# Eight output stores of the last batch on two queues instead of one

## The chip, the cores and the metric

The kernel runs on one core of a Trainium2 chip. The metric is the device time of one execution in microseconds (us), smaller being better. A core has TensorE (matrix products, "PE" in the profile, with its weight loads as "PEld"), VectorE (DVE), ScalarE (ACT), GpSimd (POOL) and SyncE (SP), each with its own instruction queue, and 16 DMA engines that carry out the transfers which these queues issue. A "q" behind an engine's name in the profile (SPq, ACTq) marks an instruction that its queue handles itself, such as the issue of a transfer.

## The reference

The inputs are q, k and v with the shape (8 batches, 8 heads, 576 positions, 64). A linear attention with an exponential feature map comes first, then a Fourier mixing over positions and channels, a normalisation and a two-layer network with a residual:

```python
q_p, k_p = (phi(q), phi(k))            # exp(proj - max|proj|), exp(-proj - max|proj|)
kv = np.einsum('bhsf,bhsd->bhfd', k_p, v)
z = np.sum(k_p, axis=2)
num = np.einsum('bhsf,bhfd->bhsd', q_p, kv)
den = np.einsum('bhsf,bhf->bhs', q_p, z)[..., None] + 1e-06
attn = num / den                       # then heads joined: x of (8, 576, 512)
mixed = np.real(fft(fft(x, axis=1), axis=2))
u = x + mixed
un = (u - mean(u)) / np.sqrt(var(u) + 1e-06)
out = u + np.maximum(un @ w_ch1, 0.0) @ w_ch2
```

The output is (8, 576, 512) in float32. Only its last line and its way to memory matter for the change.

## The kernel before, in words

The kernel goes through the eight batches as a software pipeline. Each kind of work is a generator ("stream"), and the string PLAN, one letter for a step, says in which order the steps are written into the program; each engine runs its own instructions in that order. The letter F is `forward`, the two-layer network, and PLAN ends in a run of F alone: the network of the last batch has nothing left to be mixed with.

The 576 rows of a batch are held as five chunks, `c` = 0 to 4: four of 128 rows, and chunk 4 of 64. They are not in the order of the output: because the mixing pairs row n with row 576 - n, some chunks hold rows in pairs and blocks in reverse. The tile `U` (named `X` in the profile, since it is the same tile) has the shape [128, 5, 513] and holds u; the result is added into it in place.

`forward(b)` runs in this order:

- `hidden(0, 256)`: the first layer for the positions of chunks 0 and 2; its matmuls are line 1222, and ScalarE applies the rectifier to `HT` (lines 1227 and 1229).
- `output(0)` and `output(2)`: the second layer, 16 accumulating matmuls a chunk at line 1239, then one VectorE instruction at line 1245, which scales the sum and adds it to `U`, then `store`.
- `hidden(256, S)` for the other positions, then `output(1)` and `output(3)`.
- Chunk 4. In the last batch (`b == B - 1`) its 512 columns are done as two halves of 256 (lines 1262 to 1281), each with two VectorE additions at line 1273 and two stores: 63 rows at line 1279, from ScalarE's queue for the first half and from SyncE's for the second, and one row at line 1280 from ScalarE's queue.

`store(b, U, c)` (lines 1197 to 1209) does nothing for chunk 0. For chunk 1 it stores chunks 0 and 1 together, since their rows alternate in the output: eight transfers at line 1200, one for each block of 16 partitions, each with 32 output rows of 2048 bytes (64 KB). Chunks 2 and 3 are one transfer of 256 KB each at line 1206. All of these are issued from `nc.sync`, SyncE's queue. A queue starts its instructions strictly in order: one that waits for its data, or is being issued, holds up everything behind it. Each store also has a counter that it raises when it lands; there are eight of these for the queues of SyncE and ScalarE, they are used in turn, and a store that takes one again waits until the earlier transfer with it has landed. The program ends when SyncE has seen all stores land (line 1403 in the profile) and the engines have met at a barrier.

Of the kernel before, what the change touches and what calls it, by code (L numbers as in the profile page):

```python
# [40 lines left out]
def kernel(  # L41
# [10 lines left out]
    nc = tc.nc  # L52
    B, H, S, D = q.shape
# [1143 lines left out]
    def store(b, U, c):  # L1197
        if c == 1:
            for a in range(8):
                nc.sync.dma_start(  # L1200
                    out=out[b, 225 - 32 * a:257 - 32 * a, :].rearrange("(r j) n -> r j n", j=2),
                    in_=U[16 * a:16 * a + 16, 0:2, 0:C],
                )
        elif c in (2, 3):
            rows_ = out[b, 320:576, :].rearrange("(a r j) n -> a r j n", r=16, j=2)
            nc.sync.dma_start(out=rows_[:, ::-1, 3 - c, :], in_=U[:, c, 0:C])
        elif c == 4:
            nc.sync.dma_start(out=out[b, 257:320, :], in_=U[1:64, 4, 0:C])
            nc.sync.dma_start(out=out[b, 0:1, :], in_=U[0:1, 4, 0:C])

    def forward(b):
# [23 lines left out]
        def output(c):  # L1235
            at = PLACE[c]
            po = pb.tile([128, C], F32, tag="pb", name="pso")
            for hh in range(NHH):
                nc.tensor.matmul(  # L1239
                    po[:], lhsT=HT[:, hh, at:at + 128], rhs=W2b[:, hh, :],  # L1240
                    start=(hh == 0), stop=(hh == NHH - 1),
                )
                if hh % 2 and hh < NHH - 1:
                    yield
            nc.vector.scalar_tensor_tensor(  # L1245
                out=U[:, c, 0:C], in0=po[:], scalar=scale_of[b, c], in1=U[:, c, 0:C],
                op0=ALU.mult, op1=ALU.add,
            )
            store(b, U, c)
            yield  # L1250
# [41 lines left out]
        for g in (0, 64):  # L1292
            nc.vector.scalar_tensor_tensor(
                out=U[0:64, 4, 0:C], in0=po[g:g + 64, :], scalar=scale_of[b, 4][0:64],
                in1=U[0:64, 4, 0:C], op0=ALU.mult, op1=ALU.add,
            )
        store(b, U, 4)
        yield

# [108 lines left out]
```

## Time and profile before

| what | value |
|---|---|
| time, median of 3 runs | 426.88 us (426.83 to 427.21) |
| profiled execution, its span | 426.9 us |
| TensorE matmul, busy | 400.0 us (94%) |
| TensorE weight load, busy | 255.6 us (60%) |
| VectorE, busy | 331.5 us (78%) |
| ScalarE, busy | 306.2 us (72%) |
| GpSimd, busy | 207.5 us (49%) |
| granted TensorE clock, mean | 0.993 |
| stores at line 1200 | 64, on SyncE's queue, 64 KB, 0.58 / 0.59 / 1.76 us (shortest, median, longest) |
| stores at line 1206 | 16, on SyncE's queue, 256 KB, 0.65 / 0.67 / 0.70 us |

The span reaches from the first to the last instruction of the program. Busy shares are averages over the whole span; what happens at the end of the program has to be read from the end. The time of a store here is that of its issue by the queue, not of its transfer.

### The profile page before, as it was taken

The numbers are of one execution on the slowest core, as the hardware profiler recorded it, in microseconds if no ns is written. First come the engines' busy times: TensorE is split into PE (matmuls) and PEld (weight loads), VectorE is DVE, ScalarE is ACT, GpSimd is POOL, SyncE is SP. The second block draws the span as 40 slices with busy tenths as digits, with TensorE's granted clock in tenths as the row PEclk, the third lists the DMA queues.
The fourth block names the chain that finished last, engine by engine and source line by source line (L and its number), as shares of the span: only waits on it lengthen the run. The fifth ranks groups of instructions, "written<-read, shape, count | busy, mean of one in ns | idle before, by whom it ended". The sixth has DMA issues, their size and how long they took to land.

```text
span 426.9 us, 10423 instructions
## 1 busy us (share of the span) xinstructions
PE 400.0 (94%) x4122; PEld 255.6 (60%) x4122; DVE 331.5 (78%) x682; ACT 306.2 (72%) x626; POOL 207.5 (49%) x271
## 2 busy tenths in 40 slices
PE   7787788999899999999899999999999999999993
PEld 3464466744676558555675558565766577657562
DVE  5989689698979986998779885898989786967102
ACT  7877699757984899499847888588868886353450
POOL 7983578635646077706673283734755332401000
PEclk9999899999999999999999999999999999999998
DMA  8999949993569458862899059754894151104204
GB/s 224 197 165 180 138 75 154 146 99 71 85 103 171 80 101 106 120 88 48 112 154 134 4 100 136 118 69 74 114 130 76 22 104 21 27 0 79 67 23 86
DMA packets 108699, 42.70 MB, mean 100 GB/s; under 512 B 82859, under 2 KB 103595, under 8 KB 108651
## 3 DMA queue, kind: packets, MB, share of 16 engines
q0 software_dynamic: 45936, 16.60, 36.2%
q1 hardware_dynamic: 62479, 25.31, 33.8%
q8 instruction: 32, 0.52, 0.5%
q10 hardware_dynamic: 236, 0.13, 0.1%
q14 instruction: 16, 0.13, 0.1%
HBM read 36.77 MB, written 9.44 MB: 108 GB/s over the span
## 4 chain that ended last, share of the span: by engine, by line
PE 57%; DVE 25%; ACT 8%; POOL 5%; issue 2%; DMA 2%; DVEq 0%; ACTq 0%; POOLq 0%
PE psf L1222 19%; PE pso L1239 19%; DVE R L903 4%; DVE cb L999 3%; PE kv L887 3%; DVE tg L994 3%; DVE MK L511 2%; PE pso L1286 2%; PE psD L1045 2%; PE pu L1104 2%; DMA UT<-UN 2%; DVE CEO L1034 1%; DVE MQ L555 1%; PE psq L547 1%; PE idle L1339 1%
## 5 line engine op out<-in xcount | busy, mean ns | idle before, releaser
L1222 PE MATMUL psf<-UT,W1b 128*128 128x320 bf16 (+1 forms) x1024 | 142.5, 286 | 3.2 <-DMA UT<-UN 1.5
L1239 PE MATMUL pso<-W2b,HT 128*128 128x512 bf16 x512 | 124.7, 379 | 0.0
L1222 PEld LDWEIGHTS <-W1b 128*128 128x128 bf16 x1024 | 94.0, 98 | 30.4 <-issue 4.7
L1239 PEld LDWEIGHTS <-HT 128*128 128x128 bf16 x512 | 46.4, 98 | 46.4 <-issue 2.6
L1227 ACT ACTIVATE HT<-psf 128x320 bf16<-128x320 f32 x128 | 53.5, 443 | 27.0 <-PE psf L1222 21.6
L1002 POOL TENSOR_TENSOR X<-cb,rd 128x320 f32<-128x320 f32 x56 | 41.4, 743 | 41.1 <-DVE rd L1001 39.4
L466 POOL TENSOR_TENSOR VCn<-VS,VCn 128x512 bf16<-128x512 bf16 x28 | 29.7, 1060 | 38.2 <-ACT VCn L461 35.4
L1229 ACT ACTIVATE HT<-psf 128x512 bf16<-128x512 f32 x64 | 38.0, 604 | 13.2 <-PE psf L1222 12.6
L555 DVE TENSOR_REDUCE MQ<-psq 128x8 f32<-128x1024 f32 (+1 forms) x32 | 34.3, 1085 | 14.1 <-PE psq L547 13.8
L1245 DVE SCALAR_TENSOR_TENSOR X<-pso,rs,X 128x512 f32<-128x512 f32 x32 | 23.6, 736 | 24.3 <-PE pso L1239 24.3
L497 ACT ACTIVATE KPn<-psk 128x1024 bf16<-128x1024 f32 x28 | 28.6, 1020 | 14.1 <-DVE MK L511 14.0
L497 ACT ACTIVATE KPp<-psk 128x1024 bf16<-128x1024 f32 x28 | 28.7, 1025 | 11.2 <-PE psk L491 11.1
L451 POOL TENSOR_TENSOR V4N<-VS,V4N 64x256 bf16<-64x256 bf16 x14 | 8.7, 622 | 56.1 <-ACT V4N L447 55.6
L511 DVE TENSOR_REDUCE MK<-psk 128x8 f32<-128x1024 f32 x28 | 33.9, 1213 | 1.0 <-ACT KPp L497 0.7
L1094 DVE TENSOR_TENSOR X<-pu,X 128x512 f32<-128x512 f32 (+3 forms) x49 | 23.3, 526 | 11.2 <-PE pu L1104 8.9
L466 POOL TENSOR_TENSOR VCp<-VS,VCp 128x512 bf16<-128x512 bf16 x28 | 29.6, 1058 | 0.0
L606 ACT ACTIVATE QPHP<-psh 128x1024 bf16<-128x1024 f32 x28 | 28.9, 1031 | 0.8 <-PE psh L597 0.6
L606 ACT ACTIVATE QPHN<-psh 128x1024 bf16<-128x1024 f32 x28 | 29.0, 1036 | 0.0
L1150 ACT ACTIVATE UN<-X,MV 128x512 bf16<-128x512 f32 (+1 forms) x35 | 24.5, 723 | 5.4 <-DVE MV L1175 3.1
L1174 DVE BATCH_NORM_STATS2 st<-X 128x6 f32<-128x512 f32 (+1 forms) x40 | 27.1, 677 | 0.3
L1190 POOL TENSOR_TENSOR rs<-VE,mhalf 128x5 f32<-128x5 f32 (+1 forms) x9 | 10.3, 1141 | 29.1 <-DVE VE L1189 29.1
L987 PEld LDWEIGHTS <-QPHP 128*128 128x128 bf16 x280 | 21.2, 99 | 4.6 <-DVE cb L999 1.0
(465 smaller groups left out, 819.5 us busy)
## 6 DMA issues: line engine op xcount, KB each, us to landing
out_dram<-X SPq DMA_DIRECT2D x16, 256.0 KB
out_dram<-X SPq DMA_DIRECT2D x64, 64.0 KB
QS<-in_q_dram POOLq DMA_DIRECT2D x14, 256.0 KB, 6.3
KS<-in_k_dram POOLq DMA_DIRECT2D x7, 512.0 KB, 7.5
VS<-in_v_dram POOLq DMA_DIRECT2D x14, 256.0 KB, 5.2
W1b<-in_moe_w_ch_dram POOLq DMA_DIRECT2D x1, 2048.0 KB, 13.1
W2b<-in_moe_w_ch_dram POOLq DMA_DIRECT2D x1, 2048.0 KB, 16.1
W2b<-in_k_dram SPq DMA_DIRECT2D x2, 512.0 KB
```

Of the source, the lines that this page charges most:

```text
L466: nc.gpsimd.tensor_tensor(out=VC[:, hs, :, 0:D], in0=values[b][0][:, hs, :].rearrange("p h (j d) -> p h j d", d=D), in1=VC[:, hs, :, D:D + ...
L497: nc.scalar.activation(out=KP[:, hs, :, :].rearrange("p e (jp jj) f -> p jj (e jp) f", jj=2), in_=psk[:], func=AT.Exp, scale=sgn,)
L511: nc.vector.tensor_reduce(out=MK[:, 2 * pr:2 * pr + 2, :].rearrange("p e (jp jj) -> p jj (e jp)", jj=2), in_=tiles[pr][:], axis=AX.X, op=A ...
L555: nc.vector.tensor_reduce(out=o, in_=i[:], axis=AX.X, op=ALU.max, apply_absolute_value=True)
L606: nc.scalar.activation(out=o, in_=psh[:], func=AT.Exp, scale=sgn)
L1002: nc.gpsimd.tensor_tensor(out=X[:, :, D * h:D * h + D], in0=cb[:, :, 0:D], in1=rd[:].to_broadcast([128, 5, D]), op=ALU.mult,)
L1150: nc.scalar.activation(out=UN[0:M, c, :], in_=X[0:M, c, 0:C], func=AT.Identity, scale=-1.0, bias=mv[0:M, c, 0:1],)
L1174: nc.vector.bn_stats(out=st[0:M, :], in_=X[0:M, c, 0:C])
L1222: nc.tensor.matmul(ps, lhsT=W1b[:, cc, 128 * hh:128 * hh + 128], rhs=UT[:, cc, lo:hi], start=(cc == 0), stop=(cc == NCC - 1),)
L1227: nc.scalar.activation(out=HT[:, hh, lo:hi], in_=ps, func=AT.Relu, scale=-1.0)
L1229: nc.scalar.activation(out=HT[:, hh - 1:hh + 1, lo:hi], in_=psw[:].rearrange("p (a n) -> p a n", a=2), func=AT.Relu, scale=-1.0,)
L1239: nc.tensor.matmul(po[:], lhsT=HT[:, hh, at:at + 128], rhs=W2b[:, hh, :], start=(hh == 0), stop=(hh == NHH - 1),)
```

## The change

In the last batch, the eight stores of chunk 1 are issued in turn by SyncE's queue (a = 0, 2, 4, 6) and ScalarE's queue (a = 1, 3, 5, 7). Sources, destinations and sizes are as before, and so are the stores of the seven other batches.

```diff
     def store(b, U, c):
         if c == 1:
             for a in range(8):
-                nc.sync.dma_start(
+                queue = nc.scalar if b == B - 1 and a % 2 else nc.sync
+                queue.dma_start(
                     out=out[b, 225 - 32 * a:257 - 32 * a, :].rearrange("(r j) n -> r j n", j=2),
                     in_=U[16 * a:16 * a + 16, 0:2, 0:C],
                 )
```

## The prediction, made before the changed kernel was run

> **What bounds the kernel now.** I read the chain of waits first. It runs on TensorE almost to the end, and the last compute is four short VectorE additions.
>
> ```profile
> 411.66 6.91 PE pso L1239 x32
> 418.57 1.01 PE pso L1266 x16
> ...
> 421.21 0.49 DVE X L1273
> ```
>
> The chain ends at 421.70 us, but the span is 426.9 us. The last 5.2 us hold no compute, only stores, so the timeline of that stretch comes next (columns: start, duration, engine, line, operation, count).
>
> ```profile
> 411.70 0.44 ACT L1227 ACTIVATE HT<-psf 128x320 bf16<-128x320 f32 x1
> ...
> 415.22 0.75 DVE L1245 SCALAR_TENSOR_TENSOR X<-pso,rs,X 128x512 f32<-128x512 f32 x1 [11.39 <-PE pso L1239]
> 416.00 5.11 SPq L1200 DMA_DIRECT2D out_dram<-X  x8
> ...
> 418.67 0.75 DVE L1245 SCALAR_TENSOR_TENSOR X<-pso,rs,X 128x512 f32<-128x512 f32 x1 [2.70 <-PE pso L1239]
> 419.67 2.03 DVE L1273 SCALAR_TENSOR_TENSOR X<-pso,rs,X 64x256 f32<-64x256 f32 x4 [0.25 <-PE pso L1266]
> 420.70 0.56 ACTq L1279 DMA_DIRECT2D out_dram<-X  x1
> 421.21 0.65 SPq L1206 DMA_DIRECT2D out_dram<-X  x1
> 421.30 0.67 ACTq L1280 DMA_DIRECT2D out_dram<-X  x2
> 422.63 0.31 SPq L1279 DMA_DIRECT2D out_dram<-X  x1
> ```
>
> SP issues the eight chunk 1 stores without a break from 416.00 to 421.11. Chunk 3 (the second L1245 row) is ready at 418.67 + 0.75 = 419.42, but its store sits behind them and starts at 421.21: **1.79 us lost in SP's queue**. The queue's own waits name one more thing:
>
> ```profile
> SPq L1403 <- DMA out_dram<-X: 2.5, 2, 2.2
> SPq L1279 <- DMA out_dram<-X: 0.7, 1, 0.7
> ```
>
> L1403 is the end of the program: SP stands there 2.2 us for a store to land, so transfers set the end. The second row says that SP's last store (chunk 4, second half) also waited 0.7 us for another output store. Last, the stretches of the tail (the last two numbers are the busy share of the 16 DMA engines and GB/s):
>
> ```profile
> 405.10:406.50 1.40, 1.40 (x13) 1.01 (x11) 0.00 (x0) 1.11 (x3) 0.00 (x0) 1.00 0.43 54
> 406.50:407.75 1.25, 1.25 (x11) 0.91 (x10) 0.00 (x0) 1.04 (x3) 0.00 (x0) 1.00 0.40 149
> ...
> 417.00:422.00 5.00, 3.43 (x40) 2.15 (x37) 2.68 (x5) 0.00 (x0) 0.00 (x0) 1.00 0.60 105
> 422.00:422.60 0.60, 0.00 (x0) 0.00 (x0) 0.00 (x0) 0.00 (x0) 0.00 (x0) 1.00 0.58 144
> 422.60:423.40 0.80, 0.00 (x0) 0.00 (x0) 0.00 (x0) 0.00 (x0) 0.00 (x0) 1.00 0.49 44
> 423.40:424.40 1.00, 0.00 (x0) 0.00 (x0) 0.00 (x0) 0.00 (x0) 0.00 (x0) 0.94 0.47 144
> 424.40:425.40 1.00, 0.00 (x0) 0.00 (x0) 0.00 (x0) 0.00 (x0) 0.00 (x0) 0.50 0.36 130
> 425.40:426.90 1.50, 0.00 (x0) 0.00 (x0) 0.00 (x0) 0.00 (x0) 0.00 (x0) 0.50 0.00 0
> ```
>
> The first two rows are chunk 2's store alone, issued at 403.89 with its last packet before 407.75. In the packet records that is 3.84 us from issue to the last 2048-byte packet. Chunk 3's store, of the same shape, takes 421.21 to 425.04, or 3.83 us: although chunk 1's packets run until 422.8, they cost it nothing. SP's last store is drained behind it, 0.30 us later (425.34). After that come 1.5 us without a packet (write receipts and the closing barrier), which I hold fixed. So the end today is chunk 3's issue + 3.83 + 0.30 + 1.5.
>
> **The change, step by step.** In the last batch four of the eight chunk 1 stores (a = 1, 3, 5, 7) move from SP to ACT. Batches 0 to 6 keep their order. The same 512 KB goes to the same places.
>
> 1. SP's queue. Eight issues at a pitch of (5.11 - 0.60) / 7 = 0.64 us become four: 416.00 + 3 x 0.64 + 0.59 = 418.5. SP is then free before chunk 3 is ready. Its store issues at 419.42 + 0.04 (the gap seen between 415.97 and 416.00, rounded up) = 419.46, **1.75 us earlier**. What is late next is the chunk 3 addition itself, 0.9 us after SP is free.
>
> 2. ACT's queue. ACT's last ACTIVATE ends at 412.14, and its next work is L1279 at 420.70, held by VectorE. Four stores go into this gap. No row shows this store on ACT. Nearest is ACT's w_phi load at L339, 64 rows, 0.56 and 0.61 us, and the same store on SP, 0.58 to 0.65. From below it is 0.23 (ACT's one-row store, L1280); from above 1.76, the longest of SP's 64 stores at L1200. I take 0.61 + 0.05: done at 418.6, with 2.1 us to spare before L1279. If that cover were gone (over 1.17 us a store), L1279 and both L1280 would slip by the excess. At 1.76 the four end at 423.2 and L1279 starts 2.5 us late; its last packet, 1.5 us after issue today (420.70 to 422.21), comes at 424.7, and the gain shrinks to 0.6.
>
> 3. SP's last store (L1279, second half) is held today until 422.63 by another output store, although its data is ready at 419.67 + 2.03 = 421.70. The order in which stores share completion counters shifts, so this wait may go (issue 421.73) or stay (422.63). I take that it goes; if it stays, the first packet comes 0.8 us later, as L1279's on ACT did, still no later than chunk 3's last packet plus 0.3. Worth 0.0 to 0.2.
>
> 4. Do the eight stores themselves finish in time? Here a rule speaks against the change. **The row:** from 417 to 422 the engines are busy 0.60 and move 105 GB/s, and SP offers 64 KB per 0.64 us, 102 GB/s. The engines follow the issue rate and are 40% idle. Mean packet time is 2048 B x 0.60 x 16 / 105 GB/s = 187 ns, so 256 packets need 256 x 0.187 / 16 = 3.0 us of all engines: from the first packet at 417.3 they could end at 420.3. **The rule:** the Trainium skill, "DMA: Bandwidth & Descriptors", section "Rules for kernel authors", says that spreading DMAs over SP, ACT and GpSimd gives no bandwidth, because all run on the same 16 engines, and saves only issue time, which it calls usually small beside the transfer. If 105 GB/s were all there is, the eight would still run to 422.3, chunk 3 would queue behind them, and the end would be 426.5 to 426.9. The row gives 425.4. I go by the row: issue is 5.11 us here, not small, and with ACT's L1279 beside SP's stores (422.00 to 422.60) the rate was 144 GB/s. A single store reads 16 partitions, and 64 KB in 0.6 us could also be a limit of their SBUF ports; the skill's "SBUF — State Buffer", section "Door 1", gives neighbouring blocks of 16 partitions different ports, so a pair, one per queue, would not share them. No run here shows that.
>
> 5. Chunk 3 then sends its first packets near 420.7, after or just at the end of the eight, and its last at 419.46 + 3.83 = 423.29. New beside it: ACT's first L1279, whose packets (421.5 to 422.2) today lie beside chunk 1's. It puts 7 packets of 46 ns on each of the engines that chunk 3 uses: +0.32. Then SP's last store, +0.30 as today: 423.91. TensorE and VectorE are untouched.
>
> Sum: 425.34 becomes 423.91, so 426.9 - 1.43 = 425.47; a part of step 5's 0.32 may fall into idle engine time, so I say **425.4**. The span equals the median of the runs shown (426.88), so nothing is added.
>
> **The rivals.**
>
> - *A: the engines are the bound, not the queue.* The eight stores drain at 105 GB/s whatever issues them, chunk 3's packets wait behind them until 422.3, and the time is 426.5 to 426.9. For it: the rule above, and SP's pitch and the moved bytes fit too well to tell apart. Against: 0.60 busy, 144 GB/s with two queues.
>
> - *B (slower): two queues at once slow each other's packets.* Chunk 3's first packets took 2048 x 0.49 x 16 / 44 = 365 ns (422.60 to 423.40), twice chunk 1's mean[...]. If all 256 packets of chunk 1 took X, they would end at 417.3 + 16X; at 0.33 us that is today's 422.6, and slower by 0.85 us begins at 0.38. At 0.40 chunk 3 queues 1.1 us longer: 428.0. Against: today's two-queue stretch got faster.
>
> - *C: larger gain.* If chunk 3 and the small stores interleave without cost, only SP's last store sets the end: issue 421.73 + 1.5 us to its last packet (as L1279 on ACT) = 423.2, so 426.9 - 2.1 = 424.8. This is the floor, set by VectorE.
>
> - *D: nothing moves, because another instruction holds ACT's queue.* The timeline shows none between 412.14 and 420.70; the time would be 426.9. I count it with A.
>
> **How the numbers follow.** Forecast 0.70 (425.0 to 425.9: step 5's addition at zero and ACT's stores at about 1.5 us), C 0.06, A and D 0.18, B 0.06. About 0.85 us (0.2%) is what a measurement of this kernel can tell from no change. The forecast and C are faster (0.76), A and D are the same (0.18), B is slower (0.06). The range reaches from C's floor, 424.8, into A to 426.7.
>
> **What would show it.** Right: four L1200 issues on SP and four on ACT ending near 418.6; L1206 at 419.46; DMA share in 417.3 to 420.5 above 0.8 at some 170 GB/s; the last packet near 423.9. Wrong: L1206 starting later than 420, ACT stores over 1.2 us each, or 417 to 422 still at 105 GB/s (A), or packet means over 330 ns there (B).

## The result and the profile after

| | before | after |
|---|---|---|
| time, median | 427.50 us (426.32 to 428.85, 22 runs) | 426.24 us (424.91 to 427.29, 22 runs) |
| profiled execution, span | 426.9 us | 424.3 us |
| start of the chunk 1 addition | 415.22 us | 414.05 us |
| from there to the end of the span ("the tail") | 11.65 us | 10.23 us |

The ratio of the times is 0.9965, with a 95% interval from 0.9955 to 0.9976: the change wins 1.0 to 1.9 us, 1.5 in the middle (the two medians differ by 1.26). The forecast was 425.4 within 424.8 to 426.7, and faster by 1.5.

Two things must be kept apart in this table. First, a time is not a span: the profiled execution after took 426.19 us for its span of 424.3, and in the 22 runs after 1.9 to 2.0 us lie outside the span. For the kernel before it is 1.8 us (its second profile: 427.25 for 425.5), so a tenth of the gain in the span is lost outside it, which these profiles don't explain. Second, the two profiles differ by 2.6 us, but 1.17 of that arises before the chunk 1 addition, where both programs are the same. Over the fourteen profiles of this study that addition starts anywhere from 412.66 to 415.22 us. So the tail is the measure from here on: it starts at the last event that the change can't touch. A second profile of the kernel before gave 11.54, one of the changed kernel 10.23 again, so it repeats to about 0.1 us.

The chain of waits after still ends in VectorE's short additions, at 420.52 us, with 3.8 us of stores behind them (5.2 before):

```profile
417.39 1.01 PE pso L1267 x16
...
420.04 0.48 DVE X L1274
```

The timeline of the tail after (line numbers are one higher from the changed line on; columns are start, duration, engine, line, operation, count):

```profile
414.05 0.75 DVE L1246 SCALAR_TENSOR_TENSOR X<-pso,rs,X 128x512 f32<-128x512 f32 x1 [11.39 <-PE pso L1240]
414.82 2.56 SPq L1201 DMA_DIRECT2D out_dram<-X  x4
414.83 2.86 ACTq L1201 DMA_DIRECT2D out_dram<-X  x4
...
417.50 0.75 DVE L1246 SCALAR_TENSOR_TENSOR X<-pso,rs,X 128x512 f32<-128x512 f32 x1 [2.70 <-PE pso L1240]
418.28 0.65 SPq L1207 DMA_DIRECT2D out_dram<-X  x1
418.50 2.03 DVE L1274 SCALAR_TENSOR_TENSOR X<-pso,rs,X 64x256 f32<-64x256 f32 x4 [0.25 <-PE pso L1267]
419.53 0.57 ACTq L1280 DMA_DIRECT2D out_dram<-X  x1
420.14 0.65 ACTq L1281 DMA_DIRECT2D out_dram<-X  x2
420.55 0.31 SPq L1280 DMA_DIRECT2D out_dram<-X  x1
```

SP and ACT issue four stores each, side by side. SP is idle from 417.38, and chunk 3's store starts 0.03 us after its addition ends. Measured from the start of the chunk 1 addition, it started at 5.99 us before and starts at 4.23 now: 1.76 us earlier. SP's last store has moved from 7.41 to 6.50. What it waits for has changed too, as the waits of SP's queue after say:

```profile
SPq L1404 <- DMA out_dram<-X: 1.9, 2, 1.5
SPq L1280 <- DVE X L1274: 1.5, 1, 1.5
```

It no longer waits for another store but for its data. The stretches of the tail after (the last two columns are the share of the DMA engines and GB/s):

```profile
416.10:419.10 3.00, 3.00 (x38) 2.06 (x36) 1.32 (x3) 0.00 (x0) 0.00 (x0) 1.00 0.79 175
419.10:419.50 0.40, 0.16 (x4) 0.00 (x0) 0.40 (x1) 0.00 (x0) 0.00 (x0) 1.00 0.00 0
419.50:420.50 1.00, 0.00 (x0) 0.00 (x0) 0.94 (x2) 0.00 (x0) 0.00 (x0) 1.00 0.46 53
420.50:421.50 1.00, 0.00 (x0) 0.00 (x0) 0.02 (x1) 0.00 (x0) 0.00 (x0) 1.00 0.50 147
421.50:422.10 0.60, 0.00 (x0) 0.00 (x0) 0.00 (x0) 0.00 (x0) 0.00 (x0) 1.00 0.56 205
422.10:422.80 0.70, 0.00 (x0) 0.00 (x0) 0.00 (x0) 0.00 (x0) 0.00 (x0) 1.00 0.29 100
422.80:424.30 1.50, 0.00 (x0) 0.00 (x0) 0.00 (x0) 0.00 (x0) 0.00 (x0) 0.78 0.00 0
```

The first row holds all eight chunk 1 stores: 175 GB/s in place of 105, so they are through in 3.0 us. The second row is a gap without a packet. The next three are chunk 3's store, slow at first and then fast as before (no run here shows why its first packets are slow), with the small stores of chunk 4 setting in from 7.12 us after the start of the chunk 1 addition; then come the rest of the small stores and the same 1.5 us to the end.

### The profile page after: what moved, and what is told of

Its sections match the earlier page's. It is cut to its first block, busy times and chain, and to the rows that moved or that the text cites. A ratio compares the mean times of both kernels' runs of the same rounds, so it can differ in the third digit from the quotient of the medians.

```text
span 424.3 us, 10395 instructions
## 1 busy us (share of the span) xinstructions
PE 399.3 (94%) x4093; PEld 255.9 (60%) x4122; DVE 330.8 (78%) x682; ACT 306.0 (72%) x626; POOL 207.8 (49%) x271
## 4 chain that ended last, share of the span: by engine, by line
PE 63%; DVE 22%; ACT 9%; DMA 2%; issue 2%; POOL 0%; DVEq 0%; ACTq 0%
PE psf L1223 21%; PE pso L1240 19%; DVE R L903 3%; DVE cb L999 3%; PE kv L887 3%; PE idle L1340 3%; DVE tg L994 3%; PE psD L1045 2%; DMA UT<-UN 2%; PE pso L1287 2%; PE pu L1104 2%; PE psq L547 1%; DVE MK L511 1%; PE psk L491 1%; PE psh L597 1%
## 5 line engine op out<-in xcount | busy, mean ns | idle before, releaser
L1240 PE MATMUL pso<-W2b,HT 128*128 128x512 bf16 x483 | 120.6, 379 | 1.7 <-issue 0.5
```

Of the source, the lines that this page charges most:

```text
L1240: nc.tensor.matmul(po[:], lhsT=HT[:, hh, at:at + 128], rhs=W2b[:, hh, :], start=(hh == 0), stop=(hh == NHH - 1),)
```

## The experiments

Twelve more runs were made, one profile each; with the two profiles above that makes fourteen, of eleven kernels. The main theory (Q in the expectations) says that the gain is chunk 3's store leaving SP's queue earlier. All times in this table count from the start of the chunk 1 addition. The third column is from the start of chunk 3's store to the end of its last 2048-byte packet; columns three and four come from the trace's packet records, which name the queue of a packet but not its store; packets are given to stores in the order of their queue.

| kernel | chunk 3's store starts | its transfer | last packet of all | tail |
|---|---|---|---|---|
| before, two profiles | 5.99, 5.99 | 3.83, 3.74 | 10.12, 10.03 | 11.65, 11.54 |
| one store on ACT | 5.43 | 3.69 | 9.42 | 10.96 |
| two on ACT, two profiles | 4.81, 4.83 | 4.39, 4.41 | 9.80, 9.85 | 11.31, 11.36 |
| three on ACT | 5.05 | 4.54 | 10.07 | 11.57 |
| after (four on ACT), two profiles | 4.23, 4.23 | 3.85, 3.85 | 8.68, 8.68 | 10.23, 10.23 |
| four on ACT, pairs 32 partitions apart | 4.23 | 3.81 | 8.65 | 10.20 |
| four on ACT, pairs 64 partitions apart | 4.23 | 3.85 | 8.69 | 10.25 |
| after, without chunk 4's first store | 4.23 | 3.80 | 8.40 | 9.96 |
| chunk 3 on ACT, all eight on SP | 4.24 | 4.45 | 11.43 | 12.92 |
| chunk 3 on POOL, all eight on SP | 4.82 | 4.83 (4096-byte) | 10.38 | 11.95 |
| after, and chunk 3 on POOL | 4.82 | 4.12 (4096-byte) | 9.50 | 11.19 |

**The two kernels again.**

> The changed kernel a second time, for a second profile. Tail means the time from the start of VectorE's chunk 1 addition to the end of the span: 11.7 us before (426.9 - 415.22), 10.2 us after (424.3 - 414.05). Theory Q (the gain is chunk 3's store leaving SP's queue earlier): the tail is 10.2 again within 0.1, and the start of the chunk 1 addition, which comes ahead of everything that was changed, may lie anywhere from 413 to 417. Rival N (the gain in the profile is mostly variation between executions): the tail moves as much as the start does.

> The kernel before a second time. Theory Q: tail 11.7 within 0.1, chunk 3's store again about 6.0 us after the start of the chunk 1 addition. Rival N: the tail varies by over 0.5 us.

Rival N falls: the tails repeat (10.23; 11.54 against 11.65), while the chunk 1 addition started at 413.26 and 413.94 us. Q holds for the changed kernel and for the start of chunk 3's store (5.99 again); the 11.54 lies 0.06 outside its 11.7 within 0.1.

**One, two and three stores on ACT.**

```diff
-                queue = nc.scalar if b == B - 1 and a % 2 else nc.sync
+                queue = nc.scalar if b == B - 1 and a in (7,) else nc.sync      # one
+                queue = nc.scalar if b == B - 1 and a in (5, 7) else nc.sync    # two
+                queue = nc.scalar if b == B - 1 and a in (3, 5, 7) else nc.sync # three
```

> One of the eight stores (a = 7) on ACT, seven on SP. Theory Q: SP is free 0.64 us earlier than before, so chunk 3's store starts 5.3 us after the start of the chunk 1 addition instead of 6.0, and the tail follows: 11.0 to 11.3. Rival L (what was won is the wait of SP's last store for an earlier store's counter): the tail falls to 10.8 (11.7 less that store's 0.9 us delay) if that wait is gone here, wherever chunk 3's store starts, and stays at 11.7 if it is not. Rival D (the data, not the queue): 11.7.

> Two of the eight stores (a = 5 and 7) on ACT, six on SP. Theory Q: chunk 3's store starts 4.7 us after the start of the chunk 1 addition, 1.3 us earlier than before, and the tail is 10.4 to 10.7. Rival L: 10.8 or 11.7, the same as with one store moved. Rival D: about 11.3, half of the way from before to after in steps of the stores moved (11.7 less 2/4 of 1.45 is 11.0 at the least).

> The kernel with two stores (a = 5 and 7) on ACT once more. Its first run started chunk 3's store at 4.8 us and yet had a tail of 11.3 us, because that store took 4.4 us to its last packet and not 3.8. Theory Q with a chance delay: this time 3.8 us and tail 10.7 to 10.8. Theory M (meeting: chunk 3's first, slow packets start while SP's last chunk 1 packets and ACT's small store are arriving, and this costs half a microsecond each time): 4.4 us and tail 11.3 again.

> Three of the eight (a = 3, 5, 7) on ACT, five on SP. SP is free at about 4.0 us after the start of the chunk 1 addition, before chunk 3 is ready. Theory Q: chunk 3's store starts at 4.2 us, as with four moved, and the tail is 10.2 to 10.3: the fourth store moved is worth nothing. Theory M: chunk 1's last packets on SP's queue still flow to about 6.0 us, past chunk 3's first at 5.5: chunk 3's transfer takes 4.4 us, tail 10.8. Rival D (each store moved counts): 10.6.

With one store moved, chunk 3 starts 0.56 us earlier and the tail is 0.6 to 0.7 shorter, 10.96. By its size that lies between Q's 11.0 and rival L's 10.8 and tells neither apart. L falls on other lines: SP's last store has lost its wait in this kernel and in the changed one alike, and goes at 6.51 in both, yet their tails are 0.73 apart; and its last packet comes 0.30 behind chunk 3's here, as it does before, where it went 0.9 later. The row of SP's waits for that store, with one store on ACT, names its data and no other store:

```profile
SPq L1280 <- DVE X L1274: 0.3, 1, 0.3
```

Rival D falls as well: it said 11.7 for one store. With two stores the start moved as Q says and the tail did not follow: it is 11.31, and 11.36 when run again, because chunk 3's transfer took 4.4 us and not 3.8. That isn't chance. (D's 11.3 for two stores is met in number only: chunk 3's store started 1.18 us earlier and lost 0.56 of it in its own transfer, of which D says nothing.) With three stores D's 10.6 is missed by far, at 11.57, and Q missed already at the start, 5.05 and not 4.2. The waits of SP's queue with three stores on ACT hold this row:

```profile
SPq L1201 <- DMA out_dram<-X: 1.0, 1, 1.0
```

And its timeline shows where that second went:

```profile
415.13 4.16 SPq L1201 DMA_DIRECT2D out_dram<-X  x5
415.13 2.22 ACTq L1201 DMA_DIRECT2D out_dram<-X  x3
...
419.40 0.65 SPq L1207 DMA_DIRECT2D out_dram<-X  x1
```

Five stores took SP 4.16 us instead of some 3.2: the fifth waited 1.0 us for another output store. The trace's counter records name it: SP's fifth has the same counter as ACT's second, whose last part lands at 4.36, and it starts at 4.38. The eight counters are used in turn, and the turn is fixed when the program is built, in an order of its own. By the counters' numbers, ACT's three chunk 4 stores come in it ahead of SP's fifth, which is so the eleventh and meets the counter of the third, ACT's second, while that is still on its way. With four on each queue the eight stores take the eight counters, and none waits. That split is better than three to five for a reason that the diff doesn't show.

What starts chunk 3's packets is its issue: in all eleven profiles with this store on SP the first packet comes 1.28 to 1.29 us after it, whether chunk 1's packets run right up to it (before) or a gap lies ahead of it (after). It does not wait for chunk 1's packets to end. This part of Q holds in every run; the length of the transfer is not in it.

The longer transfer with two and three stores is the half of theory M that stands. In these three profiles chunk 3's first packets come at 6.1 to 6.3 us, just when ACT's first chunk 4 store (issued at 5.48; its first packets come at 6.3 where nothing is in the way) arrives. Before, that store is ahead of chunk 3's packets, and with one store moved mostly so; with four, chunk 3's slow first packets begin at 5.5 and are more than half done by 6.3, and the small store's first packet comes at 7.12. SP's chunk 1 packets run right up to chunk 3's before and with one store as well, where the transfer takes 3.7 to 3.8 us, so they alone are not the cause. In each of the three profiles a single engine is late: in the first run with two stores seven of the eight engines report chunk 3 landed by 9.07 and one at 9.54. That the meeting of the two stores costs the half microsecond fits all of this, but it was not tried by leaving the small store out at that moment, so it stays open.

**The same split with other pairs.**

```diff
-                queue = nc.scalar if b == B - 1 and a % 2 else nc.sync
+                queue = nc.scalar if b == B - 1 and a in (2, 3, 6, 7) else nc.sync  # 32 apart
+                queue = nc.scalar if b == B - 1 and a in (4, 5, 6, 7) else nc.sync  # 64 apart
```

> Four stores on each queue as in the changed kernel, but a = 2, 3, 6, 7 on ACT, so that the two stores in flight together read blocks of partitions 32 apart (0 and 2, 1 and 3, 4 and 6, 5 and 7). Theory P (a store of 16 partitions is limited by the SBUF ports of its partitions, and these pairs share theirs): the eight move at about 105 GB/s as on one queue, last packet 7 us after the start of the chunk 1 addition instead of 5, chunk 3 is held up, tail 10.8 to 11.5. Theory I (only the issue rate limited them): 175 GB/s as in the changed kernel and tail 10.2.

> Four stores on each queue, a = 4 to 7 on ACT: pairs 64 partitions apart, which by theory P share no port, with another order of destinations. Theory P and theory I both: about 175 GB/s and tail 10.2. If it is slow like the pairs 32 apart, the cause there is not the ports but the order.

The stretch of 3.0 us from the first packet and the remainder after it, with pairs 32 apart:

```profile
416.75:419.75 3.00, 3.00 (x38) 2.06 (x36) 1.32 (x3) 0.00 (x0) 0.00 (x0) 1.00 0.91 167
419.75:420.20 0.45, 0.16 (x4) 0.00 (x0) 0.42 (x2) 0.00 (x0) 0.00 (x0) 1.00 0.39 55
```

The same two stretches with pairs 64 apart:

```profile
414.71:417.71 3.00, 3.00 (x39) 2.06 (x36) 1.31 (x3) 0.00 (x0) 0.00 (x0) 1.00 0.80 175
417.71:418.10 0.39, 0.17 (x4) 0.00 (x0) 0.39 (x1) 0.00 (x0) 0.00 (x0) 1.00 0.00 0
```

Pairs 32 partitions apart keep the engines 0.91 busy for 167 GB/s, where the changed kernel needs 0.79 for 175, and their last packet comes at 5.47 us instead of 5.04. So partitions 32 apart do get in each other's way, as theory P has it, but by 0.4 us and not by 2: that is inside the gap ahead of chunk 3, and the tail is the same (10.20). Theory P's price was far too high; theory I's 10.2 is right, its unchanged packets are not.

**Chunk 3's store taken out of the way instead.**

```diff
-            nc.sync.dma_start(out=rows_[:, ::-1, 3 - c, :], in_=U[:, c, 0:C])
+            queue = nc.scalar if b == B - 1 and c == 3 else nc.sync   # or nc.gpsimd
+            queue.dma_start(out=rows_[:, ::-1, 3 - c, :], in_=U[:, c, 0:C])
```

with all eight chunk 1 stores on `nc.sync` (the first two runs) or as in the changed kernel (the third).

> All eight chunk 1 stores stay on SP as before; instead the last batch's chunk 3 store goes to ACT. It starts 4.2 us after the start of the chunk 1 addition, as in the changed kernel, but chunk 1's packets still flow until 7.6 us. Theory Q alone (its start is all that matters): tail 10.2. Theory Q with the drain (the eight must also be out of the way): chunk 3 shares its engines for about 2 us with packets that keep them 0.60 busy, tail 10.8 to 11.5. Rival D (the doubled rate of the eight is all that matters): 11.7.

> All eight chunk 1 stores on SP as before; the last batch's chunk 3 store goes to POOL's queue, whose completion counters are its own, so the wait on chunk 3's landing that spoiled the run with that store on ACT cannot come. Theory Q with the drain: chunk 3 starts at 4.3 us but shares its engines with chunk 1's packets until 7.6; POOL's issue and start of a transfer are slower by up to 1 us; SP's last store goes at 6.5 instead of 7.4. Tail 10.4 to 11.3. Rival D (only the doubled rate of the eight counts): 11.6. If the tail is at or under 10.2, the early start of chunk 3 alone is enough.

> The changed kernel with chunk 3's store on POOL's queue as well. Theory Q: chunk 3 starts at 4.25 us as in the changed kernel, so there is nothing more to win at the issue; the tail is 10.2 if POOL is as quick as SP and up to 11.0 if it is a microsecond slower to start. If POOL spreads the store over 16 engines and not 8, its transfer shortens from 3.8 us by up to 1.2 and the tail falls to 9.7 or below.

With chunk 3's store on ACT, the timeline is this:

```profile
414.61 0.75 DVE L1247 SCALAR_TENSOR_TENSOR X<-pso,rs,X 128x512 f32<-128x512 f32 x1 [11.39 <-PE pso L1241]
415.39 8.86 SPq L1201 DMA_DIRECT2D out_dram<-X  x8
...
418.84 1.21 ACTq L1208 DMA_DIRECT2D out_dram<-X  x1
...
424.35 0.44 SPq L1281 DMA_DIRECT2D out_dram<-X  x1
```

The row of the waits of SP's queue behind the 8.86 us:

```profile
SPq L1201 <- DMA out_dram<-X: 3.8, 1, 3.8
```

Chunk 3 starts as early as in the changed kernel, and the tail is 12.92, **1.3 us longer than before**: SP's eighth chunk 1 store has the counter of chunk 3's store and waits 3.8 us for it to land, and SP's last store waits behind. No expectation had this, and the tail says nothing of theory Q or D on its own. The packets do: chunk 3's last one comes at 8.69 (4.24 + 4.45), 1.1 us earlier than before, and 0.6 later than in the changed kernel. So the early start was worth something without the doubled rate, against rival D, and chunk 1's packets in the way (seven of the eight stores; the last one was still waiting) took part of it back. The run with chunk 3 on POOL, whose counters are separate, keeps the wait out. There nothing waits for a counter, but POOL's issue starts 0.58 us later, as its row of the timeline shows:

```profile
418.37 0.72 POOL L1208 DMA_DIRECT2D out_dram<-X  x1 [25.66 <-DVE X L1247]
```

That is 4.82 us after the chunk 1 addition, still 1.2 earlier than before, and the tail is 11.95, longer than before and above what was expected. Both transfers now share the engines, and chunk 1's last packet comes at 10.08 instead of about 7.6. So in neither run did the early start of chunk 3 shorten the tail by itself. With the eight out of the way as well (the third run) the row of POOL is this:

```profile
417.68 0.72 POOL L1208 DMA_DIRECT2D out_dram<-X  x1 [25.66 <-DVE X L1247]
```

Chunk 3 again starts 4.82 us after the chunk 1 addition (at 412.86), and the tail is 11.19, 0.8 shorter than with the eight on one queue: that is what they cost in the way of this store. It is shorter than before and 1.0 longer than the changed kernel. POOL does spread the store over 16 engines, in 64 packets of 4096 bytes, but its transfer takes 4.12 us, not less than 3.8.

**Without chunk 4's first store** (its 63 rows by 256 columns are left out of the output).

```diff
-                queue.dma_start(out=out[b, 257:320, at:at + 256], in_=U[1:64, 4, at:at + 256])
+                if at:
+                    queue.dma_start(out=out[b, 257:320, at:at + 256], in_=U[1:64, 4, at:at + 256])
```

> The changed kernel without the store of chunk 4's first half (63 rows of 1 KB on ACT; these rows of the last batch are left out of the output). The prediction's step 5 charges this store with 0.32 us on the engines that chunk 3 uses: tail 9.9. Rival C (small packets interleave at no cost): 10.2.

The tail is 9.96, 0.27 shorter, which is most of step 5's 0.32, and rival C falls. Chunk 3's own transfer hardly changes (3.80 for 3.85): the small store's packets are drained behind it, and what comes earlier without them is SP's last store, whose last packet is 0.37 behind chunk 3's instead of 0.60.

## Why the prediction was right

- **What bounds the tail.** Right. Chunk 3's store waited in SP's queue, and its start set the end: 5.99 to 4.23 us, 1.76 earlier for a forecast of 1.75.
- **Step 2, ACT's queue.** The four stores took 2.86 us for a forecast of 2.6 (0.71, 0.80, 0.62 and 0.61), inside the cover of 4.7: L1280 still starts when VectorE is done.
- **Step 3, SP's last store.** Right that the wait goes (issue at 6.50 after the chunk 1 addition; 6.51 was forecast), and right that it decides nothing in this kernel. But the step priced this shift of counters at 0.0 to 0.2 us, and treated it as an affair of one small store. The run with chunk 3 on ACT shows the same mechanism at 3.8 us.
- **Step 4, the eight stores.** Right that the row decides and not the rule behind rival A: 175 GB/s against 105. That they took the 3.0 us of the packet sum (2.08 to 5.04) is in part luck. The sum supposed packets of 187 ns on engines that are never idle; the engines were 0.79 busy with packets of 148 ns, and the two differences cancel. What the stretch follows is still the issue: eight stores of 64 KB in SP's 5.11 us are 103 GB/s, and in ACT's 2.86 us 183. The clause on issue time was the useful one; it stands in the Trainium skill, "DMA: Bandwidth & Descriptors", section "Issuing engines are not separate DMA queues", which says that several issuing engines save only the time to initiate the transfers, usually small beside them. Here that time was not small, and saving it raised the rate of engines that one queue had left 40% idle. The step's other sign, 144 GB/s with two queues, was weak: ACT's small store had its last packet at 422.21, 0.2 us into that stretch, and carried 34 of the 144.
- **Step 5.** Chunk 3's transfer stayed at 3.85 us, and the last packet of all comes 0.60 behind it for a forecast of 0.62. The tail shrank by 1.42 us (1.31 against the second profile of before) for 1.43 summed.
- **The level.** Here the forecast missed: 425.4 lies 0.84 under the measured 426.24, which is outside its own 425.0 to 425.9. "The span equals the median of the runs shown (426.88), so nothing is added" rested on a chance agreement. A time lies 1.8 us above its span for the kernel before, so the profiled execution was a long one (some 428.7, an estimate from 426.9 + 1.8), and the median of three runs was a low one: that of 22 is 427.50, 0.62 higher. The other 0.22 is the gain, 1.48 forecast and 1.26 between the medians. As a time alone, 426.24 would not tell the forecast from rival A's 426.5 to 426.9; that it falls in the range is owed to the room left for A. What speaks for the forecast is the tail and its rows.
- **Rivals.** The prediction's A and D are refuted by the rate and by ACT's timeline. B's sign was not met, and packets got shorter: 2048 x 0.79 x 16 / 175 = 148 ns against 187. C's floor, a last packet 8.0 us after the chunk 1 addition (423.2 - 415.22), was not reached: chunk 3's own last packet comes at 8.08 and the last of all at 8.68, of which the small store accounts for 0.27.

## What to carry to other kernels

When a queue's solid row of store issues stands ahead of the store that ends the program, moving half of them to an idle queue is worth what that store gains in start time, as long as the moved transfers are also finished before it needs the engines; check both on the trace. A transfer moved to another queue also shifts which completion counters meet, so read the queue's waits after every such move: here the same idea, done by moving chunk 3's own store instead of four of the eight ahead of it, cost 1.3 us. Where executions vary by more than the gain, measure from the last event that the change can't reach.

## What the runs showed that was not expected

- Completion counters tie stores on different queues together: a store waited 3.8 us (chunk 3 on ACT) and 1.0 us (three on ACT) for an unrelated transfer.
- With two queues the mean packet fell from 187 to 148 ns, and partitions 32 apart in flight together raised it again (2048 x 0.91 x 16 / 167 = 179 ns).
- In the changed kernel ACT's stores beside SP's took up to 0.80 us, SP's stayed at 0.58 to 0.65.
- A store on POOL started 0.58 us later than on SP and was no faster on 16 engines than on SP's 8.
